# Hash-bucketed attention and a channel mix on one core: the third pair's q and k turned by TensorE, written PSUM banks, and a new written sequence

## The chip, the cores and the metric

The kernel runs on one core of a Trainium2 chip. The core has five engines that work side by side and wait for each other by semaphores: TensorE (PE in the profile; its weight loads are listed apart as PEld), VectorE (DVE), ScalarE (ACT), GpSimd (POOL), and SyncE (SP), which here only issues DMA transfers. The metric is the time of one execution in microseconds (us) on the device; smaller is better.

## The reference

Two blocks follow each other. First an attention whose mask comes from a hash: each row of q and k is projected on 6 random directions, the 6 signs make a bucket number, and a query sees only the keys of its own bucket. Then a channel mix with a token shift, a squared ReLU layer and a sigmoid gate.

```python
# q, k, v: (4, 8, 768, 64); proj: (64, 6); x: (4, 768, 512); w_k: (512, 1024), w_v: (1024, 512), w_r: (512, 512)
q_bits = einsum('bhsd,dk->bhsk', q, proj) > 0;  k_bits = the same of k
mask   = bucket(q_bits)[:, :, :, None] == bucket(k_bits)[:, :, None, :]
attn   = softmax(where(mask, q @ k.T / 8, -1e9));  x = heads side by side of attn @ v
x_prev = x shifted by one position, zero first
xk = mu_k * x + (1 - mu_k) * x_prev;  xr = mu_r * x + (1 - mu_r) * x_prev
out = sigmoid(xr @ w_r) * (maximum(xk @ w_k, 0) ** 2 @ w_v)
```

## The kernel before

The 32 heads are worked in 16 pairs, n = 0 to 15; four pairs make one batch b, and behind each batch its channel mix follows (`add_moe`). For a pair:

- *Loads* (`add_load`). q, k and v of both heads come from DRAM by SP's queue, three buffers each (ldq, ldv).
- *Preparation of q and k.* Each fp32 number becomes a half-precision "hi" (times 4) and the remainder "lo", side by side in 128 columns: hi on DVE, ACT or POOL (L554 to L556, L616 to L618), lo on DVE (L559, L621). The block must then be turned, so that these 128 columns lie on the partitions. There are two ways. `add_prep` (pairs 2 to 15) issues two DMA transposes on SP's queue (L563, tr). `add_prep_first` (pairs named in FIRSTS, 0 and 1) works each head and side apart: hi and lo of 384 columns, six transposes on PE into PSUM (L635, t), and a copy of 768 columns out of PSUM by DVE or ACT (L639, evt).
- *Sign rows.* PE multiplies with the projection (L587, bits), DVE takes the signs out of PSUM (L591, bx), and small DMAs put them as extra rows into the turned q and k (L599, row): two DMAs for pairs 1 to 3, four for the later ones. Pair 0 does without the DMAs: PE writes its sign products at the right partitions (L657, b) and DVE or ACT puts them into place (L663, L665, beb). With these rows, equal buckets add a constant to the score, which the exponential's bias takes off again, so unequal buckets vanish.
- *Scores* (`add_scores`). A pair has nine steps of 1024 score columns, each in two PSUM banks: PE (L708, sc), then the exponential on ACT (L712, exp). Three such double banks exist. Steps 5 to 8 are of the second head, 0 to 3 of the first, step 4 of both.
- *Times v* (`add_pv`, L736 and L741, oo): six groups of 12 matmuls per pair; DVE divides by the sum (rc, ob). For pairs 0 to 7 v is cast (va) and a sum of its rows is made in three additions (vsum, vsumb, vsumc) on DVE or POOL; later pairs subtract the mean of v (L528, mean).
- *Turn and mix* (`add_mix`): the result is turned by PE or by a DMA transpose (ot, otd), shifted (xs, xj), and mixed on DVE (df, xka, xk, xra, xr).

The channel mix of a batch has 16 blocks of the first layer (L859, kp), a ReLU on ACT or DVE (L864, L866), a square on DVE (L869), six gate blocks (L884, r, then a tanh on ACT, L887) and six blocks of the second layer (L896, v), whose product with the gate DVE makes (L903, os) before it is stored (L907, st). The very last block is made and stored in two halves of 256 columns.

What sets the order: every step is an entry of a plan with its engine, and ORDER is one written list of all entries (1386). Each engine works its own entries strictly in the order of that list. WHERE names the engine of those that can go to several. `schedule` walks the list, and for each step that needs PSUM it picks the bank that its estimates see free first, out of 0 to 5 in pairs for scores and 7 to 3 for single ones. Waits between engines follow from the data. The 512 values of mu_k and mu_r are loaded one by one into their columns (L422).

Of the kernel before, what the change touches and what calls it, by code (L numbers as in the profile page):

```python
# [16 lines left out]

LAG = {"PE": 0.21, "ACT": 0.21, "DVE": 0.15, "POOL": 0.18, "SP": 1.8, "GQ": 2.0}
# [17 lines left out]
def R(kind, n):  # L36
# [99 lines left out]
class Plan:  # L136
# [7 lines left out]
    def add(self, eng, dur, prio, fn, r=(), w=(), take=None, give=(), lag=None, name="", at=0.0, svc=0.0, off=None, tr=0, port=0, land=1.5):  # L144
# [31 lines left out]
        self.ops.append(o)  # L176
        return o

    def sequence(self):
        if ORDER:  # L180
            return [self.ops[i] for i in ORDER]
        left = {o.i: len(o.deps) for o in self.ops}
        heap = [(o.prio, o.i) for o in self.ops if not left[o.i]]
        heapq.heapify(heap)
        seq = []
        while heap:
# [73 lines left out]
def kernel(  # L260
# [13 lines left out]
    nc = tc.nc  # L274
# [690 lines left out]
```

## Time and profile before

| | |
|---|---|
| median of 3 runs | 250.7 us (248.66 to 250.73) |
| span of the profiled execution, first to last instruction (no other time of it is given) | 251.3 us |
| PE busy | 236.9 us (94%) |
| DVE busy | 195.4 us (78%) |
| ACT busy | 179.1 us (71%) |
| POOL busy | 27.9 us (11%) |
| DMA packets' time, share of 16 engines, main queue | 72.8% |

Busy time says how long an engine worked on something, not that it worked at its peak. A line Lxxx is a line of the kernel. In the lists of groups, an instruction is named by line, engine and operation, then what it writes and reads with partitions x elements, then how often; after the bar its busy time, the mean of one in ns, and the idle time of its engine before it with what ended that. In a timeline row the first number is the start, the second the length, and the bracket says how long the engine stood idle before and what released it. SPq is SP's queue of DMA issues. The granted clock of PE is given as a share of full speed, 1.00 being full.

### The profile page before, as it was taken

The page shows a single profiled execution, that of the slowest core. Times are in us where ns is not written, and L with a number is a line of the kernel's source. Part 1 is how long each engine was busy: PE and PEld are TensorE (multiplying, and loading weights), DVE is VectorE, ACT ScalarE, POOL GpSimd, SP SyncE. Part 2 cuts the span into 40 slices and gives each one's busy share as a digit, 9 for nine tenths or more (in the row PEclk, how much of TensorE's full clock was granted, in tenths as well). Part 3 has the DMA queues.
Part 4 walks back from the last instruction along what each step waited for, and adds up shares of the span by engine and source line. Part 5 has one row for each costly group of instructions (what it writes and reads, how often), then busy time and mean ns, then how long its engine had stood idle before and what let it go on. Part 6 is the DMA issues. An engine that isn't in the chain of part 4 may idle for free.

```text
span 251.3 us, 6510 instructions
## 1 busy us (share of the span) xinstructions
PE 236.9 (94%) x2609; PEld 147.6 (59%) x2609; DVE 195.4 (78%) x471; ACT 179.1 (71%) x225; POOL 27.9 (11%) x73
## 2 busy tenths in 40 slices
PE   6886799999799998999999999999999999999993
PEld 2444578876566655666467566655865654545442
DVE  3795679889788889898998999899787878376322
ACT  5596689999799978996878899988787223332220
POOL 5002240541302031100001100100000000000000
PEclk9799799999999999999999999999999999999998
DMA  6999999999989999999999996793231030022223
GB/s 187 308 178 251 220 215 191 267 249 189 213 292 241 204 293 292 273 201 269 184 333 186 184 185 158 210 230 57 90 64 44 0 128 28 13 83 86 83 85 125
DMA packets 75194, 44.56 MB, mean 177 GB/s; under 512 B 55524, under 2 KB 70172, under 8 KB 75164
## 3 DMA queue, kind: packets, MB, share of 16 engines
q1 hardware_dynamic: 74028, 44.15, 72.8%
q8 instruction: 20, 0.33, 0.6%
q10 hardware_dynamic: 1136, 0.01, 0.3%
q14 instruction: 10, 0.08, 0.1%
HBM read 24.12 MB, written 6.29 MB: 121 GB/s over the span
## 4 chain that ended last, share of the span: by engine, by line
PE 75%; DMA 11%; DVE 8%; SPq 3%; ACT 1%; issue 1%; DVEq 0%
PE ps_all L708 19%; PE ps_all L896 17%; PE ps_all L859 13%; PE ps_all L741 12%; PE ps_all L884 8%; DMA nat<-in_k_dram 5%; PE ps_all L587 4%; DMA nat<-in_q_dram 3%; DMA a<-bx 2%; DMA os<-in_moe_w_k_dram 1%; DVE nh L559 1%; DVE nh L556 1%; PE ps_all L736 1%; ACT pt L712 1%; PE ps_all L794 1%
## 5 line engine op out<-in xcount | busy, mean ns | idle before, releaser
L712 ACT ACTIVATE pt<-ps_all 128x1024 bf16<-128x1024 f32 x144 | 138.8, 1040 | 21.1 <-PE ps_all L708 19.8
L708 PE MATMUL ps_all<-a 128*128 128x512 f16 (+3 forms) x408 | 80.6, 318 | 5.1 <-DMA a<-bx 3.9
L708 PEld LDWEIGHTS <-a 128*128 128x128 f16 x408 | 35.3, 98 | 26.7 <-DMA a<-bx 4.7
L859 PE MATMUL ps_all<-xk,wk 128*128 128x384 bf16 x256 | 49.0, 326 | 0.9 <-DVE kr L866 0.9
L896 PE MATMUL ps_all<-wv,k 128*128 128x512 bf16 (+1 forms) x200 | 45.9, 370 | 0.6 <-DVE os L903 0.6
L741 PEld LDWEIGHTS <-pt 128*128 128x128 bf16 x1152 | 42.1, 98 | 6.9 <-issue 1.1
L741 PE MATMUL ps_all<-va,pt 128*128 128x65 bf16 x1152 | 43.9, 194 | 0.0
L859 PEld LDWEIGHTS <-wk 128*128 128x128 bf16 x256 | 24.5, 98 | 17.6 <-issue 1.6
L896 PEld LDWEIGHTS <-k 128*128 128x128 bf16 x200 | 19.4, 98 | 20.6 <-issue 0.7
L864 ACT ACTIVATE kr<-ps_all 128x384 bf16<-128x384 f32 x33 | 15.8, 493 | 19.2 <-DVE k L869 12.7
L887 ACT ACTIVATE rs<-ps_all 128x512 f32<-128x512 f32 x24 | 14.2, 603 | 20.9 <-PE ps_all L884 19.0
L559 DVE SCALAR_TENSOR_TENSOR nh<-nat,nh 128x768 f16<-128x768 f32 x28 | 27.3, 976 | 1.1 <-ACT nh L554 0.6
L903 DVE SCALAR_TENSOR_TENSOR os<-rs,ps_all 128x512 f32<-128x512 f32 (+1 forms) x25 | 16.5, 662 | 14.7 <-PE ps_all L896 9.9
L869 DVE TENSOR_TENSOR k<-kr 128x384 bf16<-128x384 bf16 x64 | 21.5, 350 | 3.7 <-ACT kr L864 3.5
L884 PE MATMUL ps_all<-wr,xr 128*128 128x512 bf16 x96 | 23.8, 379 | 0.0
L866 DVE TENSOR_SCALAR kr<-ps_all 128x384 bf16<-128x384 f32 x31 | 17.1, 555 | 8.3 <-PE ps_all L859 6.6
L758 DVE TENSOR_TENSOR ob<-ps_all,rc 128x384 bf16<-128x384 f32 (+1 forms) x36 | 18.3, 511 | 1.0
L884 PEld LDWEIGHTS <-xr 128*128 128x128 bf16 x96 | 9.0, 98 | 10.0 <-ACT kr L864 0.3
L587 PE MATMUL ps_all<-a,p0g 128*32 128x256 f16 (+1 forms) x180 | 13.4, 276 | 1.3 <-DMA a<-nh 1.3
L556 DVE TENSOR_SCALAR nh<-nat 128x768 f16<-128x768 f32 x22 | 12.3, 557 | 3.0 <-DMA nat<-in_q_dram 2.5
L587 PE MATMUL ps_all<-a,p1g 128*32 128x256 f16 (+1 forms) x180 | 12.9, 273 | 0.0
L841 DVE TENSOR_TENSOR xr<-tm,xt 128x768 bf16<-128x768 f16 (+1 forms) x18 | 9.4, 520 | 0.4
(94 smaller groups left out, 187.4 us busy)
## 6 DMA issues: line engine op xcount, KB each, us to landing
vn<-in_v_dram SPq DMA_DIRECT2D x16, 384.0 KB
out_dram<-os SPq DMA_DIRECT2D x23, 256.0 KB
nat<-in_k_dram SPq DMA_DIRECT2D x15, 384.0 KB
nat<-in_q_dram SPq DMA_DIRECT2D x15, 384.0 KB
wst<-in_moe_w_k_dram SPq DMA_DIRECT2D x2, 512.0 KB
wst<-in_moe_w_r_dram SPq DMA_DIRECT2D x2, 512.0 KB
wst<-in_moe_w_v_dram SPq DMA_DIRECT2D x2, 512.0 KB
a<-bx SPq DMA_DIRECT2D x48, 9.0 KB
```

The lines of the kernel that those rows point to most:

```text
L559: nc.vector.scalar_tensor_tensor(out=nh[:, :, D:P], in0=nat.rearrange("p j (c d) -> p (j c) d", d=D), scalar=QS, in1=nh[:, :, 0:D], op0=AL ...
L587: nc.tensor.matmul(ps[g_ * wid : (g_ + 1) * wid, 0:FW], w_[:, m_ - 1 - x : m_ - 1 - x + wid], a_t[sa][:, i, x % NFOLD * FW : (x % NFOLD + ...
L708: nc.tensor.matmul(ps[:, lo - s * STEP : hi - s * STEP], side_a["k"][sa][:, j, jc * P : (jc + 1) * P], side_a["q"][sa][:, j, q0 : q0 + hi ...
L712: nc.scalar.activation(out=pt_t[sp][:, s * STEP : (s + 1) * STEP], in_=ps_t[plan.slot[nm]], func=AF.Exp, bias=EBIAS, scale=ESC)
L741: nc.tensor.matmul(oo[:, (ic - c0) * 65 : (ic - c0) * 65 + 65], pt_t[sp][:, o : o + P], va_t[sa][:, j, jc, 0 : D + 1], start=(not uc and i ...
L758: nc.vector.tensor_tensor(out=ob_t[so][:, c0:c1, j * D : (j + 1) * D], in0=oo[:, :, 0:D], in1=rc_t[sr][:, 1, c0:c1].unsqueeze(2).to_broadc ...
L859: nc.tensor.matmul(ps[:, 0:HALF], wk_sb[:, d, fc * P : (fc + 1) * P], xk_t[mx[d]][:, h * HALF : (h + 1) * HALF], start=(d == 0), stop=(d = ...
L866: nc.vector.tensor_scalar(out=kr_t[sk], in0=sm(nm)[:, 0:HALF], scalar1=0.5 ** 0.5, scalar2=0.0, op0=ALU.mult, op1=ALU.max)
L869: nc.vector.tensor_tensor(out=k2_t[s2][:, h * HALF : (h + 1) * HALF], in0=kr_t[sk], in1=kr_t[sk], op=ALU.mult)
L884: nc.tensor.matmul(sm(nr), xr_t[mx[d]][:, c * P : (c + 1) * P], wr_sb[:, d, :], start=(d == 0), stop=(d == NDC - 1))
L896: nc.tensor.matmul(sm(nv)[:, lo:hi], k2_t[(b * NFC + fc) % NK2][:, c * P : (c + 1) * P], wv_sb[:, fc, lo:hi], start=(fc == 0), stop=(fc == ...
L903: nc.vector.scalar_tensor_tensor(out=os_t[so][:, lo:hi], in0=rs_t[s1][:, lo:hi], scalar=1.0, in1=sm(nv)[:, lo:hi], op0=ALU.add, op1=ALU.mult)
```

## The change

- FIRSTS becomes (0, 1, 2): pair 2's q and k are prepared by `add_prep_first` too. Two DMA transposes, two whole hi and two whole lo go; four hi and four lo of 384 columns, four groups of six PE transposes and four copies out of PSUM come.
- mu_k and mu_r are loaded as eight rows of 128 values, turned by one PE matmul with an 8 x 8 identity (made on POOL), and taken out of PSUM by one DVE instruction, in place of two loads of single values and two DVE instructions.
- SLOT names the PSUM bank of every operation; `schedule` only looks it up. Single operations may now lie in banks 0 to 7.
- ORDER is new (1397 entries), and so is the engine of many entries (WHERE). POOL has 103 entries in place of 67, among them most of the v sums and twelve casts of q or k; ACT has 217 in place of 227, DVE 437 in place of 455, PE 464 in place of 459, SP 176 in place of 178.
- The plan's durations and times of some entries change, which nothing reads any more. STEPS, ROWD, ROW_ACT and NWARM2 are options, all empty or zero. The second half of the last block is declared to follow the first (nv, 0).

How some lists begin or end, by the names above, before and then after:

```
PE  t0k10 t0q01 t0q00 t0q10 t0k01 t0k00 b0k10 b0q10 b0k00 b0k01 t1k10 b0q00 sc0_6 sc0_8 b0q01 t1q00 sc0_7 t1k00 sc0_5 t1q10 sc0_3 sc0_2 bits1 sc0_1 sc0_4 sc0_0 bits2 sc1_0 ...
PE  t0k10 t0q10 b0k10 t0q01 t0q00 b0q10 t0k00 t0k01 b0q01 sc0_7 sc0_6 b0q00 b0k00 sc0_5 t1q10 b0k01 t1q00 t1k00 t1k10 sc0_3 sc0_4 bits1 sc0_2 t2k10 sc0_1 t2q00 t2k00 t2q10 sc0_8 sc0_0 bits2 sc1_8 ...
DVE hi0k1 lo0k1 lo0q0 lo0q1 hi0k0 lo0k0 evt0q01 evt0q00 hi1k1 evt0k00 lo1k1 lo1k0 hi2q lo2q beb0q10 ...
DVE hi0k1 lo0k1 hi0q1 lo0q1 evt0k10 lo0q0 evt0q10 lo0k0 evt0q01 hi1q0 evt0q00 beb0q10 lo1q1 beb0q01 lo1q0 hi2q1 vsum0 hi1k1 lo1k1 vsum0b lo1k0 evt1q10 beb0q00 evt1k00 evt1k10 hi3q lo2k1 va1 lo2k0 bx1 lo2q0 evt2k10 lo2q1 evt2q00 evt2k00 evt2q10 ...
SP  ldq0k1 ldq0q0 ldq0q1 ldq0k0 ldq1k ldq2q ldq2k ldq1q ldq3q ldq3k tr2 ldq5q tr2 ldv0 ldq4q ldq4k row1 row1 ldv1 ldv2 row2 row2 tr3 tr3 ...
SP  ldq0k1 ldq0q1 ldq0q0 ldq0k0 ldq1q ldv0 ldq2q ldq1k ldq3q ldq2k ldv1 ldq4q ldv2 ldq3k ldq4k ldv3 row1 row1 ldv4 ldq5k ldq5q ldq6q row2 row2 tr3 tr3 tr4 tr4 ...
PE  ... r3_3 r3_5 v3_4 v3_5 (first half, 2 groups) v3_5 (second half, 2 groups)
PE  ... v3_5 (first half, 1) r3_3 v3_5 (first half, 2) r3_4 r3_5 v3_5 (second half, 2 groups) v3_4 (2 groups)
```

The diff, without the lists:

```diff
+BANKS = {"sc": 2, "s3": 3, "sm": 1}
-    FIRSTS = (0, 1)
+    FIRSTS = (0, 1, 2)
+    STEPS = {}
+    NWARM2 = 0
+    ROWD = ()
...
     def schedule(self):
...
+        used, held = set(), {}
+        order = [self.ops[i] for i in ORDER]
         for o in order:
             if o.take is not None:
-                choices = [(max(t, *(bank_free[b] for b in bs)), k, i, bs) for k, (i, bs) in enumerate(choices) if not any(used[b] for b in bs)]
-                t, _, self.slot[name], bs = min(choices)
+                name, size = o.take[1], BANKS[o.take[0]]
+                self.slot[name] = SLOT[name]
...
-    for t, src, key in ((muk, moe_mu_k, "muk"), (mur, moe_mu_r, "mur")):
-        def f_mu(t=t, src=src):
-            with nc.allow_non_contiguous_dma(reason="512 values"):
-                nc.scalar.dma_start(out=t, in_=src.rearrange("(c p) -> p c", p=P))
+    add("POOL", 0.3, -2.2, lambda: make_identity(nc, id8), w=["id8"], name="id8")
+    for i_, src in enumerate((moe_mu_k, moe_mu_r)):
+        add("ACT", 0.42, -19.0, lambda i_=i_, src=src: nc.scalar.dma_start(out=mu8[i_ * NDC : (i_ + 1) * NDC, :], in_=src.rearrange("(c p) -> c p", p=P)),
+            w=[("mu8", i_)], at=0.75, svc=0.05, off=1.5, land=1.05, name=f"ldmu{i_}")
+    add("PE", 0.12, 1.0, lambda: nc.tensor.matmul(sm("mu")[:, 0 : 2 * NDC], mu8, id8, start=True, stop=True),
+        r=["id8", ("mu8", 0), ("mu8", 1)], w=[("mu",)], take=("sm", "mu", 0), name="mu")
+    add("DVE", 0.08, 1.3, lambda: nc.vector.tensor_scalar(out=mu_t, in0=sm("mu")[:, 0 : 2 * NDC], scalar1=-1.0, scalar2=None, op0=ALU.add),
+        r=[("mu",)], w=["muk", "mur"], give=["mu"], name="muv")
...
-                        r=[("wv", fc) for fc in range(4 * g, 4 * g + 4)] + [...],
+                        r=[("wv", fc) for fc in range(4 * g, 4 * g + 4)] + [...] + ([(nv, 0)] if lo and g == 0 else []),
```

More of the change, by code (lines that the diff above doesn't have):

```diff
@@ L177, in add @@
         return o
[L179 to L186, printed above, removed]
-            o = self.ops[heapq.heappop(heap)[1]]
-            seq.append(o)
-            for s in o.succ:
-                left[s] -= 1
-                if not left[s]:
-                    heapq.heappush(heap, (self.ops[s].prio, s))
-        return seq
@@ L195, in moved @@
-    @staticmethod
-    def moved(t, work):
-        return t + work * (1.25 if t < 9.3 else 1.0)
-    def schedule(self):
-        free = {e: 0.0 for e in ("PE", "ACT", "DVE", "POOL", "SP")}
-        bank_free = [0.0] * 8
-        used = [False] * 8
-        count = {"sc": 0, "sm": 0, "moe": 0}
-        held = {}
-        dma_free = tr_free = after = 0.0
-        port = [0.0, 0.0]
-        queue = []
-        order = self.sequence()
+    def schedule(self):
+        used, held = set(), {}
+        order = [self.ops[i] for i in ORDER]
@@ L209, in schedule @@
         for o in order:
-            e = "POOL" if o.eng == "GQ" else o.eng
-            if o.svc and o.eng != "GQ":
-                queue.append(o)
-            t = max([free[e], o.at] + [queue[-9].vis if o.svc and o.eng != "GQ" and len(queue) > 8 else 0.0] + [self.ops[d].own if self.ops[d].eng == o.eng and not self.ops[d].svc else self.ops[d].vis for d in o.deps])
             if o.take is not None:
-                cls, name, moe = o.take
-                if count[cls] >= self.most[cls] or (moe and count["moe"] >= self.moe_most):
+                name, size = o.take[1], BANKS[o.take[0]]
@@ L221, in schedule @@
-                held[name] = (cls, bs, moe)
-                for b in bs:
-                    used[b] = True
-                count[cls] += 1
-                count["moe"] += moe
-            o.start = t
-            dur = o.dur
-            if o.port:
-                dur += max(0.0, port[e == "DVE"] - t)
-                port[e != "DVE"] = t + dur
-            if e == "SP":
-                dur += after
-                after = 0.3 * o.tr
-            if o.tr:
-                dma_free += 0.5 * (dma_free > t)
-                dur = max(dur, dma_free - 1.0 - t, tr_free + 0.1 - t)
@@ L237, in schedule @@
-            o.took = dur
-            free[e] = t + dur
-            lag = o.lag
-            if o.svc:
-                first = max(t + o.off, dma_free)
-                dma_free = self.moved(first, o.svc)
-                lag = max(0.9, dma_free + o.land - t - dur)
-                if o.tr:
-                    tr_free = dma_free
-            o.own = t + dur + 0.1 * (e in ("DVE", "ACT"))
-            o.vis = t + dur + lag
-            for name in o.give:
-                cls, bs, moe = held.pop(name)
-                for b in bs:
-                    used[b] = False
-                    bank_free[b] = o.vis
-                count[cls] -= 1
-                count["moe"] -= moe
@@ L255, in schedule @@
-        self.end = max(o.start + o.took for o in order)
+                used |= held[name]
+            for name in o.give:
+                used -= held.pop(name)
         return order
```

75 lines of the change are left out of this document (46 added, 29 removed), and 200 rows, old and new, of tables (ORDER, SLOT, WHERE).

## The prediction, made before the result was known

> **What bounds the kernel now.** I read the page's busy shares first, then three stretches, then what TensorE (PE) waited for.
>
> ```profile
> PE 236.9 (94%) x2609; PEld 147.6 (59%) x2609; DVE 195.4 (78%) x471; ACT 179.1 (71%) x225; POOL 27.9 (11%) x73
> ...
> 18.00:22.70 4.70, 4.70 (x59) 3.13 (x56) 3.68 (x6) 4.36 (x6) 0.00 (x0) 1.00 1.07 287
> 22.70:26.60 3.90, 0.02 (x2) 0.00 (x0) 1.58 (x5) 0.62 (x1) 1.67 (x2) 1.00 0.81 240
> 26.60:32.80 6.20, 6.17 (x71) 4.29 (x72) 3.59 (x6) 4.28 (x5) 1.08 (x2) 0.72 0.99 186
> ...
> 32.40:60.00 27.60, 27.59 (x485) 21.81 (x487) 23.97 (x63) 27.53 (x30) 8.86 (x18) 1.00 1.00 224
> 60.00:180.00 120.00, 117.39 (x1460) 74.62 (x1453) 106.99 (x264) 103.28 (x123) 12.21 (x26) 1.00 0.96 220
> ...
> PE ps_all L708 <- DMA a<-bx: 3.9, 1, 3.9
> ...
> PE ps_all L587 <- DMA a<-nh: 1.3, 2, 1.0
> ...
> PE ps_all L859 <- DVE kr L866: 0.9, 1, 0.9
> ```
>
> In a stretch, the numbers are its length, then busy time of PE, weight loads, DVE, ACT and POOL, then granted clock, DMA share and GB/s. PE is the bound: of the 120 us from 60 to 180 it is busy 117.39. From 32.4 to 60 ACT (27.53 of 27.60) is as full as PE. So no gain is to be had where PE is full, except by less PE work, and the change adds some. What can be won is PE's waits, and the largest stands at 22.7: 3.9 us in which the scores of the second pair wait for the sign rows (a<-bx). Behind it the granted clock is 0.72 for 6.2 us, so another 0.28 x 6.2 = 1.7 us of PE work is lost. The waits of 0.4 to 1.0 us between 12 and 18 left the clock at 1.00:
>
> ```profile
> 12.00:18.00 6.00, 4.50 (x38) 2.58 (x37) 5.81 (x12) 5.38 (x7) 0.00 (x0) 1.00 0.86 164
> ...
> 9.12 0.36 DVE L618 TENSOR_SCALAR nh<-nat 128x384 f16<-128x384 f32 x1 [1.51 <-DMA nat<-in_k_dram]
> 10.59 0.56 DVE L556 TENSOR_SCALAR nh<-nat 128x768 f16<-128x768 f32 x1
> 11.18 0.96 DVE L559 SCALAR_TENSOR_TENSOR nh<-nat,nh 128x768 f16<-128x768 f32 x1
> 12.17 0.95 DVE L665 TENSOR_SCALAR a<-ps_all 6x768 uint16<-6x768 uint16 x1
> ...
> 13.18 1.03 PE L708 MATMUL ps_all<-a 128*128 128x512 f16 x6 [0.99 <-DVE a L665]
> 26.63 1.70 PE L708 MATMUL ps_all<-a 128*128 128x512 f16 x7 [3.91 <-DMA a<-bx]
> ...
> 12.17 1.55 SPq L563 DMA_TRANSPOSE a<-nh  x1
> 15.62 2.04 SPq L563 DMA_TRANSPOSE a<-nh  x1
> 20.45 2.36 SPq L599 DMA_DIRECT2D a<-bx  x2
> ...
> L599 SPq DMA_DIRECT2D a<-bx x54: 721/752/1562, 20.4 to 177.4; - x54
> ```
>
> **The first scores** (start 13.18). They wait for the sign bits of the first pair's q, written by DVE at 12.17, and that DVE instruction stands behind the cast and remainder of the third pair's q (10.59 and 11.18). In the new sequence those two are gone from there; ahead of the sign bits stand the second pair's q cast and one 384-wide copy. That cast needs the fifth load, which landed at 9.12 (then k, now q). So 9.12 + 0.36 + 0.35 + 0.95 = 10.8: scores start 2.4 us sooner.
>
> **The second pair's scores** (start 26.63). From there DVE's written list sets the pace. Up to the rows' input (bx1) it holds six 384-wide remainders, two 384-wide sign copies, two 384-wide casts, three 768-wide copies, a 768 cast of q, one of v, and two v sums. With these rows:
>
> ```profile
> L621 DVE SCALAR_TENSOR_TENSOR nh<-nat,nh 128x384 f16<-128x384 f32 x8 | 4.4, 560 | 0.9 <-ACT nh L616 0.8
> L639 DVE COPY a<-ps_all 128x768 f16<-128x768 f16 x2 | 1.0, 552 | 0.0
> L509 DVE TENSOR_TENSOR vt<-va 128x390 f32<-128x390 bf16 x7 | 3.9, 557 | 0.0
> L512 DVE TENSOR_TENSOR vt<-vt 128x130 f32<-128x130 f32 x4 | 1.2, 294 | 2.3 <-POOL vt L509 2.2
> L591 DVE TENSOR_SCALAR bx<-ps_all 128x256 uint16<-128x256 uint16 x15 | 6.3, 421 | 3.8 <-PE ps_all L587 3.0 <-ACT pt L712 0.6
> ...
> 34.41 0.51 PE L794 MATMUL ps_all<-idb,ob 128*128 128x128 bf16 x6
> 34.75 1.15 PE L708 MATMUL ps_all<-a 128*128 128x128 f16 x8
> ...
> 35.91 1.43 PE ps_all L587 x24
> 41.18 0.44 PE ps_all L708 x4
> 99.73 0.77 PE ps_all L587 x24
> 101.05 0.65 PE ps_all L859 x4
> ```
>
> 6 x 0.56 + 2 x 0.555 (as the 384-wide copy out of PSUM of L866, below) + 2 x 0.36 + 3 x 0.55 + 2 x 0.56 + 0.557 + 0.29 = 8.8; bx1 starts at 10.8 + 8.8 = 19.6 and ends at 20.0. Then two remainders and four copies of the third pair: 6 x 0.55 = 3.3, to 23.3; PE's bits2 (24 matmuls, 1.43 us in the chain of waits, whose rows are the last four) to 24.7. DVE instructions overlap a little (two of L639, 552 ns each, are busy 1.0 us together): over some 24 of them at least 1 us less, 23.7. PE itself has less in between: after bits1 (ends about 18.8) four score steps of 0.44 and the third pair's transposes, 4 x 0.34 (six of L794 start at 34.41, what follows them at 34.75), end before 22. The added PE work, 24 transposes or 1.4 us, thus lies in a wait. The rows can end later than that: bx1 at 19.5 and two median issues of 0.75 make 21.0. Before, 3.8 us passed from their issue's end (22.81) to the scores, with ten loads and two transposes ahead; now twelve loads and no transpose are. Between 2 us and that 3.8 I take 3.1, which gives 24.1, **2.5 us sooner** than 26.63. Bounds: 23.2, if the overlap is twice as large; 26.6, if the first row's issue takes its 1.56 again and the landing longer.
>
> **The clock.** By the same walk PE's longest single wait there is about 0.9 us, for the second pair's k remainder, of the kind that left 1.00 between 12 and 18. So the **1.7 us** go too; the other bound is nothing.
>
> Against this speaks a sentence of the Trainium skill (TensorE: Matmul & The Clock Gate, Part 4: PE-mode transpose): transposes do not count as PE-busy for the clock gate, so filling the wait with them would not keep the clock. In this trace transposes among matmuls from 14.57 to 17 ran at 1.00, and none runs alone for 3 us; it is a rival below with a small chance.
>
> **Middle, 24 to 240.** Counts by engine, from the two lists: POOL goes from 67 to 103 operations (13 more first v sums, 9 more second and third ones, 8 whole and 4 half q/k casts, 2 weight casts; small ones left out). ACT loses 6 relus, 4 casts, 2 weight casts. DVE loses 22 v sums and 6 casts, and gains 6 relus and 6 copies.
>
> ```profile
> L509 POOL TENSOR_TENSOR vt<-va 128x390 f32<-128x390 bf16 x1 | 0.8, 847 | 0.1
> L512 POOL TENSOR_TENSOR vt<-vt 128x130 f32<-128x130 f32 x4 | 1.7, 436 | 11.7 <-DVE vt L509 11.7
> L501 POOL CAST va<-vn 128x768 bf16<-128x768 f32 x6 | 5.6, 930 | 25.6 <-DMA vn<-in_v_dram 19.3 <-PE ps_all L741 6.1 <-PE ps_all L859 0.2
> L866 DVE TENSOR_SCALAR kr<-ps_all 128x384 bf16<-128x384 f32 x31 | 17.1, 555 | 8.3 <-PE ps_all L859 6.6 <-issue 0.4
> L559 DVE SCALAR_TENSOR_TENSOR nh<-nat,nh x28: 947/955/1459, 11.2 to 160.3; 128x768 f16<-128x768 f32 x28
> ```
>
> POOL: 13 x 0.85 + 9 x 0.44 + 10 x 0.93 + 2 x 1.24 = 27 us more (casts at the 0.93 of the cast row, by width; at the two-operand rate of L509, 0.847/390 us, the ten would be 1.7 each and the sum 34). DVE: 13 x 0.557 + 9 x 0.29 + 6 x 0.557 - 6 x 0.555 - 6 x 0.5 = 7 us less; ACT some 8 less. None of that is PE's time; it is slack, and I give it the 0.9 us wait for L866. Against it, the sequence now issues the transposes of pairs 7 and 8 in one block of four, after four weight loads instead of two. The last of them leaves two issues, 4.1 us by the 2.04 above, after the second; PE has 3.4 us between (bits7 0.77, two first-layer blocks of 0.65, three score steps of 0.44). I keep the old 1.3 us wait for transposes and add **0.5**; bounds: -1.3 (all hidden) and +4 (two more transposes uncovered). The loading vectors mu, now turned by one small matmul, add 0.2 on PE (more than one transpose's 0.06, less than six's 0.34).
>
> Costed at nothing: the options that the diff adds are empty, so the score step stays 1024 wide and no row takes another queue; the written banks only name which read a block has to wait for, and with three score pairs and five single banks as before I see no row that would price another choice; the second head's turn at PE comes first in both lists for most pairs. ACT hides the two turned mu loads: they are issued on its queue between instructions, and mu is needed only when the first mixing starts.
>
> **The end.** The sequence ends differently.
>
> ```profile
> 245.35 0.60 ACT L887 ACTIVATE rs<-ps_all 128x512 f32<-128x512 f32 x1 [0.81 <-DVE os L903]
> 245.67 0.69 DVE L903 SCALAR_TENSOR_TENSOR os<-rs,ps_all 128x512 f32<-128x512 f32 x1 [0.41 <-PE ps_all L896]
> 246.60 0.42 DVE L903 SCALAR_TENSOR_TENSOR os<-rs,ps_all 128x256 f32<-128x256 f32 x1 [0.24 <-PE ps_all L896]
> 247.07 1.03 PE L896 MATMUL ps_all<-wv,k 128*128 128x256 bf16 x8 [0.57 <-DVE os L903]
> ```
>
> Before, the second half of the last block waits 0.57 us until DVE has read the first half out of the same bank. Now that second half follows r3_5 directly on PE: r3_5, then ACT's tanh 0.60, then os 0.42, with hand-overs of 0.03, 0.03 and 0.05, make a wait of 1.13. And the last block is a whole one: os 0.69 instead of 0.42, a store of 256 instead of 128 KB (0.45 at the 287 GB/s of 18 to 22.7; nothing, if latency alone counts). I take 0.56 + 0.27 + 0.4 = **1.2 us** lost; bounds 0.6 and 1.8.
>
> **The sum**: -2.5 - 1.7 - 0.9 + 0.5 + 0.2 + 1.2 = -3.2. (The 2.4 us of the first scores are not a term of their own: they are in the 24.1.) The profiled execution's span is 251.3, 0.6 above the median of 250.7; I apply the difference to the median: **247.5 us**. About 1% (2.5 us) is what a measurement of this kernel can tell from no change. The own range of this case, with the bounds of its steps, is 245 to 249.3.
>
> **Rivals.**
> - *The wait only moves* (0.16). The second pair's rows land late again, or its bits wait for casts now on POOL (hi1q1, hi1k0), which DVE's remainders follow in order. Then the 2.5 and the 1.7 are not won: 247.5 + 4.2 = 251.7. For it: loads fill the queue (share 1.07 just before). Against: no transposes ahead.
> - *Vector becomes the bound; slower* (0.14). An operation on POOL and one on DVE stretch each other: L559 took 1.459 at most against 0.955 while POOL cast v at 27.6. From 60 to 180 DVE is busy 106.99 of 120; with 5 us freed there and, by the lists, 18 of the 27 new POOL us falling there, full blocking makes 107 - 5 + 18 = 120. From that point on DVE's own waits for PE, some 6 us (L866 alone 6.6 over the whole span), come on top: 247.5 + 6 = 253.5. Against: most of the 28 L559 stayed near 0.955. The Trainium skill (SBUF — State Buffer, SBUF: two separate sides) has such a rule, one of the two holds a shared port for its whole instruction and the other blocks; the stretched rows agree that it happens.
> - *More slack than counted* (0.16). Second pair at 23.2 and all transposes hidden: 247.5 - 0.9 - 1.3 - 0.5 = 244.8.
> - *Transposes do not hold the clock* (0.05): 247.5 + 1.7 = 249.2.
>
> **Chances.** Forecast 0.49, of which two thirds lie under 248.2 (1% under the median): faster 0.34 + 0.16 = 0.50. Within 1%: 0.15 + 0.05 + 0.14 (of the moved wait) = 0.34. Slower: 0.14 + 0.02 = 0.16. The range leaves out most of the slow rival and the best of the fast one: 244.0 to 252.5.
>
> **What would show it.** Right: first scores near 10.8 and those of pair two near 24; no L708 wait on a<-bx over 1 us; clock 1.00 from 24 to 36; an L896 wait on os of about 1.1 us and a last store later after PE. Wrong: L559 or L837 well over their medians on average; PE waits on POOL or L621 above 1 us; bits8 waiting more than 2 us for a<-nh.

## The result and the profile after

The changed kernel takes **258.7 us** (median of four executions, 258.13 to 262.10) against 249.8 for the kernel before in the same comparison: a ratio of **1.042, interval 1.034 to 1.049**. It is slower by some 9 to 10 us where I had forecast 3 us less. (The ratios here leave out executions that took over 1.5% longer than the fastest of the same kernel; the medians hold them, so the two can differ, mostly by some tenths of a per cent.)

Something on the base first. In every execution that lists both, the time lies 1.7 to 2.1 us above the span. So the profile that the forecast read (span 251.3) is of an execution of about 253.1 us, longer than every timed one then (248.66 to 250.73). I had a second profile taken of the unchanged kernel (run `again`, below: span 247.8, time 249.73), and compare with that one from here on. The 8.5 us between the spans 247.8 and 256.3 are what is to be explained.

The busy times of the whole span, the second profile of before first, then the changed kernel:

```profile
PE 235.7 (95%) x2609; PEld 147.4 (59%) x2609; DVE 194.7 (79%) x471; ACT 179.0 (72%) x225; POOL 27.5 (11%) x73
```

```profile
PE 238.2 (93%) x2618; PEld 148.2 (58%) x2635; DVE 197.5 (77%) x453; ACT 172.1 (67%) x215; POOL 77.3 (30%) x110
```

VectorE has 18 operations fewer and is busy 2.8 us longer; POOL has 37 more and is busy 50 us longer.

Stretches of the kernel before, second profile (length, then busy time of PE, weight loads, DVE, ACT, POOL, then granted clock, DMA share, GB/s):

```profile
6.00:12.00 6.00, 3.90 (x27) 2.21 (x25) 4.25 (x11) 2.70 (x5) 0.56 (x4) 0.80 1.03 335
12.00:24.00 12.00, 11.15 (x104) 6.52 (x102) 10.10 (x18) 10.69 (x13) 0.66 (x1) 0.96 0.85 203
24.00:36.00 12.00, 10.28 (x144) 7.45 (x145) 9.13 (x18) 9.71 (x12) 4.96 (x11) 1.00 1.10 231
...
0.00:60.00 60.00, 53.44 (x724) 36.93 (x725) 46.76 (x106) 50.05 (x58) 16.51 (x49) 0.97 0.99 236
60.00:180.00 120.00, 118.22 (x1467) 75.84 (x1465) 106.19 (x265) 104.09 (x124) 10.66 (x23) 1.00 0.89 215
```

The same stretches of the changed kernel:

```profile
6.00:12.00 6.00, 5.03 (x32) 2.19 (x30) 4.99 (x11) 3.98 (x8) 2.63 (x8) 1.00 1.07 360
12.00:24.00 12.00, 10.08 (x116) 7.01 (x117) 11.87 (x23) 9.45 (x12) 10.76 (x17) 1.00 0.70 237
24.00:36.00 12.00, 11.22 (x161) 8.07 (x158) 8.47 (x15) 10.72 (x12) 4.82 (x7) 1.00 1.11 228
...
0.00:60.00 60.00, 53.35 (x709) 36.42 (x710) 46.20 (x99) 48.21 (x56) 33.12 (x62) 1.00 0.93 235
60.00:180.00 120.00, 113.94 (x1433) 73.34 (x1440) 101.50 (x232) 104.13 (x124) 43.94 (x48) 1.00 0.87 200
```

Read three things. The clock is 1.00 throughout, so that part of the start came as forecast; but up to 60 us PE is busy for the same 53.4 us in both, and in the changed kernel that has to hold 24 transposes and the mu product more (the higher clock is worth about 1.2 us of it, see `again` below). The start is thus no gain. From 60 to 180 PE idles 6.1 us (120 - 113.94) instead of 1.8: 4.3 us lost in the middle. And VectorE is less busy there than before (101.50 against 106.19), while POOL is busy four times as long.

PE's transposes of q and k, the second profile of before first, then the changed kernel with its mu product:

```profile
L635 PE MATMUL ps_all<-idh,nh 128*128 128x128 f16 x48 | 4.5, 241 | 2.7 <-DVE nh L621 2.7
```

```profile
L630 PE MATMUL ps_all<-idh,nh 128*128 128x128 f16 x72 | 6.6, 235 | 2.2 <-DVE nh L616 2.0
...
L405 PE MATMUL ps_all<-id,tm 8*128 8x8 f32 x2 | 0.4, 262 | 0.0
```

PE's waits of the changed kernel (what it waited for: us in total, times, longest), and below them the first score steps of the first two pairs and the end in the timeline (start, length, in brackets the idle time before and its releaser):

```profile
PE ps_all L703 <- DMA a<-bx: 2.7, 5, 1.0
PE ps_all L630 <- DVE nh L616: 2.0, 4, 0.8
PE ps_all L854 <- DVE ob L753: 1.8, 1, 1.8
...
PE ps_all L570 <- POOL p0g L399: 1.1, 1, 1.1
PE ps_all L891 <- DVE os L898: 1.1, 1, 1.1
...
PE ps_all L570 <- DMA a<-nh: 0.6, 1, 0.6
PE ps_all L511 <- POOL vs L498: 0.5, 1, 0.5
```

```profile
10.29 1.02 PE L703 MATMUL ps_all<-a 128*128 128x512 f16 x5 [0.64 <-DVE a L660]
...
24.25 1.04 PE L703 MATMUL ps_all<-a 128*128 128x256 f16 x5
...
249.74 2.76 PE L891 MATMUL ps_all<-wv,k 128*128 128x256 bf16 x15 [1.14 <-DVE os L898]
...
252.60 0.69 DVE L898 SCALAR_TENSOR_TENSOR os<-rs,ps_all 128x512 f32<-128x512 f32 x1 [1.36 <-PE ps_all L891]
```

No single wait is large. The loss is many small ones, of which the largest, 1.8 us at 140.9, shows how they arise: PE waits for DVE's division (ob), DVE waits 2.5 us for a DMA transpose of the older ob, and that transpose was issued on SP's queue only at 134.91, behind loads and rows. Two waits are for POOL itself, where before had none. The longer of them shows best what a full POOL does:

```profile
34.93 2.13 POOL L539 TENSOR_SCALAR nh<-nat 128x768 f16<-128x768 f32 x1
37.14 1.62 POOL L492 TENSOR_TENSOR vt<-va 128x390 f32<-128x390 bf16 x1
...
39.33 0.20 POOL L399 COPY p0g<-p 128x6 f16<-128x6 f16 x1
...
39.58 0.29 PE L570 MATMUL ps_all<-a,p0g 128*32 128x256 f16 x4 [1.15 <-POOL p0g L399]
```

PE's sign product needs the projection in the layout p0g. That copy takes POOL 0.20 us, but in POOL's list it stands behind a cast of 2.13 us and a v sum of 1.62, and PE waits 1.15 us for it.

Groups of operations on DVE and POOL (count | busy, mean ns of one | idle before), the changed kernel first, then the second profile of the kernel before:

```profile
L539 POOL TENSOR_SCALAR nh<-nat 128x768 f16<-128x768 f32 x8 | 17.4, 2176 | 25.5 <-DMA nat<-in_q_dram 10.4 <-DVE mc L524 8.7 <-DMA a<-nh 6.1
L492 POOL TENSOR_TENSOR vt<-vn 128x384 f32<-128x384 f32 x8 | 9.6, 1195 | 29.9 <-DMA vn<-in_v_dram 29.8
...
L492 POOL TENSOR_TENSOR vt<-va 128x390 f32<-128x390 bf16 x6 | 6.5, 1084 | 0.8 <-DVE va L484 0.5
L484 POOL CAST va<-vn 128x768 bf16<-128x768 f32 x6 | 5.7, 957 | 6.9 <-DMA vn<-in_v_dram 5.4 <-PE ps_all L736 1.5
L613 POOL TENSOR_SCALAR nh<-nat 128x384 f16<-128x384 f32 x4 | 5.3, 1327 | 3.5 <-DMA nat<-in_q_dram 2.2 <-DMA nat<-in_k_dram 1.1
...
L542 DVE SCALAR_TENSOR_TENSOR nh<-nat,nh 128x768 f16<-128x768 f32 x26 | 26.4, 1018 | 0.3 <-POOL nh L539 0.2
L864 DVE TENSOR_TENSOR k<-kr 128x384 bf16<-128x384 bf16 x64 | 24.3, 399 | 4.2 <-ACT kr L859 3.8
```

```profile
L559 DVE SCALAR_TENSOR_TENSOR nh<-nat,nh 128x768 f16<-128x768 f32 x28 | 27.3, 975 | 1.1 <-ACT nh L554 0.6
L869 DVE TENSOR_TENSOR k<-kr 128x384 bf16<-128x384 bf16 x64 | 21.6, 352 | 3.7 <-ACT kr L864 3.5
```

A q or k cast on POOL takes 2.18 us where DVE needs 0.56, and DVE's own operations are longer beside it: 64 squares at 399 ns instead of 352 are 3.0 us alone.

### The profile page after: what moved, and what is told of

Read it like the earlier page. It is cut to its first block, busy times and chain, and to the rows that moved or that the text cites. A ratio compares the mean times of both kernels' runs of the same rounds, so it can differ in the third digit from the quotient of the medians.

```text
span 256.3 us, 6565 instructions
## 1 busy us (share of the span) xinstructions
PE 238.2 (93%) x2618; PEld 148.2 (58%) x2635; DVE 197.5 (77%) x453; ACT 172.1 (67%) x215; POOL 77.3 (30%) x110
## 4 chain that ended last, share of the span: by engine, by line
PE 56%; DVE 16%; DMA 10%; issue 6%; ACT 4%; POOL 4%; SPq 2%; DVEq 0%; POOLq 0%; ACTq 0%
PE ps_all L891 14%; PE ps_all L854 12%; PE ps_all L703 10%; PE ps_all L736 8%; PE ps_all L879 7%; DMA a<-nh 5%; ACT pt L707 4%; PE ps_all L570 3%; DVE nh L542 3%; DMA xt<-ob 2%; DMA nat<-in_q_dram 2%; DVE nh L616 2%; POOL nh L539 2%; DMA k<-in_moe_w_v_dram 1%; DVE nh L539 1%
## 5 line engine op out<-in xcount | busy, mean ns | idle before, releaser
L736 PEld LDWEIGHTS <-pt 128*128 128x128 bf16 x1152 | 43.5, 97 | 8.7 <-issue 0.9
L703 PEld LDWEIGHTS <-a 128*128 128x128 f16 x408 | 34.2, 97 | 23.8 <-issue 4.6
L736 PE MATMUL ps_all<-va,pt 128*128 128x65 bf16 x1152 | 45.5, 193 | 0.1
L882 ACT ACTIVATE rs<-ps_all 128x512 f32<-128x512 f32 x24 | 14.2, 596 | 24.1 <-PE ps_all L879 19.9
L859 ACT ACTIVATE kr<-ps_all 128x384 bf16<-128x384 f32 x27 | 13.0, 490 | 21.8 <-PE ps_all L854 11.5
L864 DVE TENSOR_TENSOR k<-kr 128x384 bf16<-128x384 bf16 x64 | 24.3, 399 | 4.2 <-ACT kr L859 3.8
L542 DVE SCALAR_TENSOR_TENSOR nh<-nat,nh 128x768 f16<-128x768 f32 x26 | 26.4, 1018 | 0.3 <-POOL nh L539 0.2
L539 POOL TENSOR_SCALAR nh<-nat 128x768 f16<-128x768 f32 x8 | 17.4, 2176 | 25.5 <-DMA nat<-in_q_dram 10.4
L861 DVE TENSOR_SCALAR kr<-ps_all 128x384 bf16<-128x384 f32 x37 | 20.3, 553 | 5.9 <-PE ps_all L854 4.9
L492 POOL TENSOR_TENSOR vt<-vn 128x384 f32<-128x384 f32 x8 | 9.6, 1195 | 29.9 <-DMA vn<-in_v_dram 29.8
L879 PEld LDWEIGHTS <-xr 128*128 128x128 bf16 x96 | 9.3, 98 | 10.8 <-DVE xr L836 0.8
```

Of the source, the lines that this page charges most:

```text
L539: e.tensor_scalar(out=o, in0=x, scalar1=QS, scalar2=None, op0=ALU.mult)
L542: nc.vector.scalar_tensor_tensor(out=nh[:, :, D:P], in0=nat.rearrange("p j (c d) -> p (j c) d", d=D), scalar=QS, in1=nh[:, :, 0:D], op0=AL ...
L703: nc.tensor.matmul(ps[:, lo - s * w : hi - s * w], side_a["k"][sa][:, j, jc * P : (jc + 1) * P], side_a["q"][sa][:, j, q0 : q0 + hi - lo], ...
L736: nc.tensor.matmul(oo[:, (ic - c0) * 65 : (ic - c0) * 65 + 65], pt_t[sp][:, o : o + P], va_t[sa][:, j, jc, 0 : D + 1], start=(not uc and i ...
L861: nc.vector.tensor_scalar(out=kr_t[sk], in0=sm(nm)[:, 0:HALF], scalar1=0.5 ** 0.5, scalar2=0.0, op0=ALU.mult, op1=ALU.max)
L864: nc.vector.tensor_tensor(out=k2_t[s2][:, h * HALF : (h + 1) * HALF], in0=kr_t[sk], in1=kr_t[sk], op=ALU.mult)
```

## The experiments

Ratios are to the kernel before on the same chip in the same comparison; 0.01 is 2.5 us. Theory A was: POOL's long operations and their stretching of VectorE are the loss. Theory B: the written sequence, whatever engine does what. Theory C: turning the third pair on PE.

**again**: the kernel before, unchanged.

> The kernel before, unchanged, profiled a second time. Its first profiled execution had a span of 251.3 us; the changed kernel's 258.13 us has a span of 256.3, so a span lies about 1.8 us under the time, and 251.3 would be a time of 253.1, above all timed runs of the kernel before (248.66 to 250.73). Theory 'the profile was untypical': span 247 to 249, the wait of the second pair's scores for a<-bx clearly under 3.9 us or the clock behind it above 0.9, so that 2 to 4 of the 4.2 us that the forecast won at the start were not there to win. Rival 'typical': the wait is again 3.9 and the clock again 0.72, span 250 to 251.5.

Ratio 1.000 (0.996 to 1.004), median 249.7. The profile was untypical: span 247.8, and

```profile
25.41 1.46 PE L708 MATMUL ps_all<-a 128*128 128x512 f16 x7 [1.95 <-DMA a<-bx]
```

the wait was 1.95 us instead of 3.91, and behind it the clock was 1.00; low clock stood between 6 and 24 us, worth some 1.2 us (0.2 of 3.9 and 0.04 of 11.2).

**poolback** and **hiback**: the changed kernel with operations taken off POOL again.

```diff
 # poolback: 49 entries of v sums, v casts and, from the fourth pair on, q/k casts as in the kernel before
-    "vsum5": "POOL", "vsum5b": "POOL", "hi8q": "POOL", "hi13q": "POOL", ...
+    "vsum5": "DVE",  "vsum5b": "DVE",  "hi8q": "DVE",  "hi13q": "ACT", ...
 # hiback: only the 12 q/k casts that were on POOL
```

> The changed kernel with its written sequence and banks, but every v sum, every v cast and every q and k cast from the fourth pair on, on the engine that has it before (49 of 87 entries differ). POOL's busy time falls from 77 to some 45 us, VectorE's counts rise by about 10 us and its stretch shrinks. Theory A (POOL's slow casts and sums, and their stretching of VectorE, are the loss): 250 to 253 us, ratio to the kernel before 1.00 to 1.015. Theory B (the written sequence itself is the loss, whatever engine does what): 257 to 260, ratio 1.03 to 1.04.

> The changed kernel with only its 12 q and k casts on POOL (2.18 us for 128x768) given back to VectorE (8) and ScalarE (4); v sums stay on POOL. Theory A with the casts as the main part: 252 to 256 us. Theory A with the v sums as the main part, or theory B: 257 to 260.

poolback: **262.6 us, ratio 1.052 (1.043 to 1.061)**; hiback: 260.5, ratio 1.046 (1.034 to 1.058). Neither is faster than the change; poolback's median is 3.9 us longer. Its largest wait of PE was for a v sum, now on DVE:

```profile
PE ps_all L511 <- DVE vs L498: 2.7, 1, 2.7
```

The test wasn't clean for theory A: it freed POOL but loaded DVE and ACT in a sequence in which their entries had been placed without that work. (hiback also moved four casts of the start, where PE then waited 2.9 us for a remainder.)

**bpool**, **bvs**, **bhi**, **bpcut**: the same engines, the other way round, in the kernel before.

```diff
 # bpool: 45 entries as in the changed kernel; bvs: the 32 v sums alone; bhi: the 13 q/k casts alone
-    "vsum5": "DVE",  "vsum5b": "DVE",  "hi8q": "DVE",  "hi13q": "ACT", ...
+    "vsum5": "POOL", "vsum5b": "POOL", "hi8q": "POOL", "hi13q": "POOL", ...
 # bpcut: bpool, and on POOL only
+    E = 4                                # v sums, from the fifth pair on
+    o, x = o[:, 0:1, :], x[:, 0:1, :]    # q/k casts: 1 of 12 chunks
```

> The kernel before, in its own sequence, with the engines of the changed kernel for the v sums and for the q and k casts from the fourth pair on (45 entries differ; POOL 28 -> some 65 us). Theory A: 254 to 258 us, ratio 1.02 to 1.035, with VectorE's 128x768 remainder above 1.00 us on average. Theory B: 249 to 251.5, ratio 0.995 to 1.007.

> The kernel before, its own sequence, with only the v sums on the engines of the changed kernel (32 entries: 27 go to POOL, 5 come back). Both kinds together gave 256.7 us, ratio 1.030. If it goes by POOL's busy time, v sums hold half: 252.5 to 254, ratio 1.012 to 1.018. If the chain cast, remainder, transpose, rows is what counts, v sums cost little: 250 to 251.5.

> The kernel before, its own sequence, with only the q and k casts from the fourth pair on as in the changed kernel (13 entries, 8 of them to POOL at 2.15 us). By POOL's busy time: 252.5 to 254. If VectorE's remainders waiting for POOL's casts (8.1 us in the run with both kinds) are the cost: 255 to 257, ratio 1.022 to 1.03.

> Both kinds moved in the sequence of before, with POOL's casts cut to 1 of 12 chunks and its v sums from the fifth pair on to 4 of 64 columns (that part of the computation is left out). If the durations on POOL are the cost of the move: 248 to 251 us, ratio 0.993 to 1.005. If it is the order on POOL's queue and the added hand-overs, whatever an operation takes: 254 to 257.

bpool: **256.7 us, ratio 1.030 (1.021 to 1.039)**; bvs: 254.3, 1.017 (1.007 to 1.028); bhi: 253.9, 1.018 (1.009 to 1.026). So the move, with no other part of the change's sequence, costs 3%, each kind by itself about half of that. In bpool VectorE's remainders stood 8.1 us behind POOL's casts:

```profile
DVE nh L559 <- POOL nh L556: 8.1, 3, 3.7
```

But bpcut, with the durations on POOL cut, stayed at 255.4, **ratio 1.026 (1.017 to 1.036)**: in that sequence most of the cost, as far as the intervals tell, is not how long an operation takes. The wait above falls to 0.9 us there, and PE's waits stay. POOL, too, works its list in order, and what now stands on it queues behind entries that themselves wait:

```profile
POOL nh L562 <- DMA nat<-in_q_dram: 26.4, 4, 8.1
POOL xt L784 <- DVE tm L843: 24.5, 1, 24.5
POOL vt L511 <- DMA vn<-in_v_dram: 21.8, 6, 6.0
```

That this queueing is what delays DVE and PE in bpcut is argued from these rows, not shown by a run of its own. And it has a rival: the four runs did not move operations alone. In the kernel before, `schedule` picks PSUM banks by its estimates, and these go by the engine of each entry. By the kernels' own plans, 78 of the 339 blocks that need a bank lie in another one in bpool than before (48 in bvs, 76 in bhi), and bpcut has bpool's very banks. PE's waits for exponentials, first in `again`, then in bpool, then in bpcut:

```profile
PE ps_all L708 <- ACT pt L712: 0.3, 1, 0.3
```

```profile
PE ps_all L708 <- ACT pt L712: 3.4, 5, 1.2
PE ps_all L587 <- ACT pt L712: 1.2, 1, 1.2
```

```profile
PE ps_all L714 <- ACT pt L718: 3.6, 6, 1.2
PE ps_all L593 <- ACT pt L718: 1.2, 1, 1.2
```

Neither scores nor sign products read what an exponential writes, so these are waits for a bank to be read out. The sign product of 1.2 us is that of the eighth pair, which lies in bank 5 in these two runs and in bank 6 before. The waits are as long with the durations cut as without. How much of the 3% are the banks and how much the queue on POOL, no run shows.

Sequence and engines, set against each other (ratio to the kernel before):

| | engines of before | engines of the change |
|---|---|---|
| sequence of before | 1.000 | 1.030 (bpool) |
| sequence of the change | 1.052 (poolback) | 1.042 |

(The exchanged entries are nearly the same: v sums and q/k casts from the fourth pair on, in poolback the v casts too.) Each sequence has its lower number with the engines that it was written with, but the intervals of 1.042 and 1.052 overlap, and 1.030 holds other banks too. So theory A and theory B can't be told apart by exchanging engines: the two were chosen together. What can be taken away without unbalancing a list is the duration of an operation.

**short**, **shorthi**, **shortv**: the changed kernel with POOL's durations cut as in bpcut (both kinds, the 8 whole q/k casts, the v sums).

> The changed kernel, same sequence, engines and banks, but POOL's operations are cut: a v sum on POOL from the fifth pair on adds 4 of its 64 columns, a q or k cast on POOL from the fourth pair on turns 1 of its 12 chunks (the rest of the tile keeps older values, so that part of the computation is left out). POOL's busy time falls from 77 to some 40 us and its holding of VectorE with it; nothing else moves. Theory A (POOL's durations and their stretching of VectorE are the loss): 250 to 253.5 us, ratio 1.00 to 1.015, VectorE's 128x768 remainder back to 0.96 us on average. Theory B (the written sequence, with its queue of transfers, is the loss): 256 to 258.5, ratio 1.025 to 1.035.

> As the run with POOL's work cut, but only the 8 whole q and k casts on POOL are cut (1 of 12 chunks each, the rest of the computation of these casts is left out): some 14 of the 29.5 us. If the loss is POOL's own lateness in one chain (cast, remainder, transpose, rows), the casts hold the most of it: 254 to 255.5 us. If it is the stretching of VectorE, it goes by POOL's busy time, about half of 5.4 us: 255.5 to 256.5.

> The other half: only the v sums on POOL are cut (4 of 64 columns from the fifth pair on; that part of the sums is left out), some 16 of the 29.5 us. Stretching by busy time: 255.5 to 256.5. Lateness of the casts as the main part: 257 to 258.5.

short: **253.3 us, ratio 1.020 (1.009 to 1.032)**, against 1.042 (1.034 to 1.049) of the change: the intervals don't meet (barely), so in this sequence, with the same banks, POOL's durations are worth some 5 us. The ratio lies between what I expected by theory A (up to 1.015) and by theory B (from 1.025). Its rows:

```profile
PE 235.6 (94%) x2618; PEld 147.8 (59%) x2635; DVE 189.9 (75%) x453; ACT 171.9 (68%) x215; POOL 47.8 (19%) x110
...
L548 DVE SCALAR_TENSOR_TENSOR nh<-nat,nh 128x768 f16<-128x768 f32 x26 | 26.0, 1002 | 0.1
L870 DVE TENSOR_TENSOR k<-kr 128x384 bf16<-128x384 bf16 x64 | 21.5, 356 | 4.4 <-ACT kr L865 4.0
...
60.00:180.00 120.00, 115.42 (x1432) 74.53 (x1440) 96.95 (x238) 103.65 (x123) 19.16 (x45) 1.00 0.86 198
```

With POOL at 47.8 instead of 77.3 us, VectorE's busy time falls from 197.5 to 189.9, though its count is the same 453, and the squares are back at 356 ns. (The remainder at 1002 ns is not back at 0.96, as I had expected.) shorthi gives 254.7 (1.024, 1.017 to 1.031) and shortv 254.6 (1.021, 1.013 to 1.029): each half gives back nearly all that both do, so my expectation that the gain goes by busy time is wrong. Nor does it go by VectorE's stretch: VectorE's busy time falls by 3.4 us in shorthi (194.1), 4.6 in shortv (192.9) and 7.6 in short, which adds up, while the gains of 4.4, 5.2 and 5.3 us by the ratios don't, as far as intervals of 2 to 3 us either way tell. The 1.15 us wait for p0g fits the lateness on POOL: it is there with the casts uncut (shortv, 1.5) and isn't listed in short or shorthi. Which share the stretch has stays open. Of the 4.7 us between the spans of the change and of short (256.3 and 251.6), 2.1 are idle time of PE and 2.6 are busy time (238.2 and 235.6).

**hy24** and **hy70**: the changed kernel's order and engines up to 24 or 70 us, then the rest as before.

```diff
-ORDER = [ ...the changed kernel's list... ]
+ORDER = [ ...its entries up to the second pair's first scores (hy70: the first layer)...,
+          ...all others in the kernel before's order... ]
```

> The changed kernel up to the first scores of the second pair (third pair turned by PE, mu turned by PE, the new start), then what is left in the order and on the engines of the kernel before. Theory A and theory B both lose it all after 24 us, so 245 to 248 us, ratio 0.98 to 0.99, if the start's gain of the forecast is real; 249 to 250 (ratio 0.995 to 1.005) if the profile of before was untypical there. Theory C (the third pair by PE and the mu matmul cost it): 254 to 258, ratio 1.02 or more.

> The changed kernel's order and engines up to PE's first layer of the first block (about 70 us), then what is left in the order and on the engines of the kernel before. With the same join as the run cut at 24 us, which gave 254.6 us. If the loss of the middle arises before 70 us: 255 to 258. If it arises behind 70 us: 251 to 254.6.

hy24: median 254.6 us, ratio 1.017 (1.007 to 1.028); hy70: 256.8, 1.033 (1.024 to 1.043). The start alone, followed by before's rest, is slower than before. Part of that is the join: PE waits 1.7 us for a v sum that the list now reaches late. hy70 does not date the loss, only that it isn't all behind 70 us. Neither run is the changed kernel up to its join, for the banks were chosen anew: of 344 blocks, 230 lie in another bank than in the changed kernel in hy24 and 212 in hy70. It shows in hy70's waits of PE:

```profile
PE ps_all L732 <- ACT pt L736: 3.6, 7, 1.1
...
PE ps_all L659 <- DVE a L689: 1.9, 1, 1.9
```

The second stands at 15.14 and about half of the first between 31 and 47 us, where order and engines are still those of the changed kernel. The changed kernel's list of PE waits has none for an exponential. Up to 60 us the two still keep pace: the score step that waits for its rows starts at 59.76 in hy70 and at 59.43 in the changed kernel.

**third** and **third2**: the kernel before with two parts of the change alone, the third pair by PE and the mu product.

```diff
-    FIRSTS = (0, 1)
+    FIRSTS = (0, 1, 2)
 # DVE, third:  bx1 | hi2 lo2 x4 | copies x4 | bx2 | hi3 lo3 x2 | v sums of pair one | hi4 ...
 # DVE, third2: bx1 | hi2 lo2 x4 | copies x4 | v sums of pair one | hi3 lo3 | bx2 | hi3 lo3 | hi4 ...
```

> The kernel before, its order and engines, with two parts of the change alone: the third pair's q and k are turned by PE (its casts and remainders on VectorE behind the second pair's rows) and the mixing vectors by one small matmul. In the forecast's sum the first scores come 2.4 us sooner and the second pair's scores 2.5 us; against the kernel before's second profile (wait for a<-bx of 1.9 us instead of 3.9) about half of that is left: 248 to 250 us, ratio 0.99 to 1.00. If the added transposes (24, some 1.7 us of PE) find no wait to lie in, 251 to 253, ratio 1.005 to 1.015.

> The kernel before, its order and engines, with the third pair's q and k turned by PE and the mixing vectors by one matmul, as in the run before of this kind, but with the first pair's v sums ahead of the third pair's copies' followers, all four turns of the third pair ahead of the second pair's scores, and the second pair's rows ahead of the next load. The 4.0 us wait for the v sums and the turn queued behind the scores' wait go; the second pair's scores start near 22 us instead of 25.4. If the start's gain is real: 247 to 249.5 us, ratio 0.985 to 1.00. If VectorE's added copies (6 of 0.55 us) only move the wait to the third pair's rows: 250 to 252.

third was badly laid out: 257.4 us at the least, 260.6 in the median, PE waiting 4.0 us for the first pair's v sums, which I had left behind the third pair's work on DVE. third2 mended that and still gives, against 247 to 252 us expected, **254.7, ratio 1.026 (1.019 to 1.033)**, although its second pair's scores start 3.4 us sooner than in the second profile (25.41):

```profile
21.96 1.03 PE L732 MATMUL ps_all<-a 128*128 128x512 f16 x5
...
32.34 0.51 PE L818 MATMUL ps_all<-idb,ob 128*128 128x128 bf16 x6 [1.94 <-DVE ob L782]
...
0.00:60.00 60.00, 52.48 (x704) 37.16 (x705) 46.24 (x107) 47.84 (x56) 17.35 (x48) 0.97 0.81 212
```

The 3.4 us are spent again within ten: PE comes to the first pair's turn at 30.4 and waits until DVE, which is busy without a break from 18.0 to 34, has divided it. By 60 us PE has worked 1 us less than before, and more of it is added work. All but 15 of 339 blocks lie in the banks of before, so theory C holds in this list: the third pair by PE costs here, and does not gain. In the change's own sequence it was not tried alone.

**t2cut**: third2 with the third pair's 8 casts and remainders cut to 1 of 6 chunks.

> The second kernel with the third pair turned by PE in the sequence of before (254.7 us), but its 8 casts and remainders on VectorE do 1 of 6 chunks (the rest keeps older values, that part of the computation is left out): some 2.9 us less on VectorE between 18 and 22 us, about as much as turning by PE had added there; the 24 transposes of PE and the 4 copies stay. If VectorE's queue between 12 and 36 us is what takes the gain of the start back: 250.5 to 252.5 us. If PE's added transposes or the later rows of pairs three and four do: 254 to 255.5.

The four executions took 251.6, 252.0, 255.9 and 256.4 us. The ratio, 1.012 (1.002 to 1.022), goes by the two shorter ones; the median of all, 254.0, is hardly under third2's 254.7, and the interval overlaps third2's, which begins at 1.019. So whether taking some 3 us from VectorE gives anything back stays open, and with it whether VectorE's queue is what takes the gain of the start.

**tailb** and **shorttail**: the last blocks in before's order, in the changed kernel and in short.

```diff
-PE: v3_5  r3_4  r3_5  v3_5 v3_5  v3_4 v3_4
+PE: r3_4  r3_5  v3_4 v3_4  v3_5  v3_5 v3_5
```

> The changed kernel with the last blocks in the order of the kernel before (whole block 4 first, the two halves of block 5 last). The forecast's own term for the end, 1.2 us (a wait of 1.13 instead of 0.57, a longer last read and store): 257.0 to 257.8 us against 258.3 to 259.1. If the later store was hidden, 258 to 259.

> POOL's work cut as in the first run of that kind (parts of the v sums and of the q and k casts left out) and the last blocks in the order of the kernel before. If the two causes add: 253.3 - 1.2 = 252.1 us (251.5 to 252.7), and what is left to the kernel before, about 2 us, belongs to the start and the rest of the sequence. If the end's order only matters while the middle is late: 253 to 254.

tailb: 257.3 us, ratio 1.033 (1.027 to 1.038). That is 1.4 us under the change, about the size forecast, but the intervals overlap. shorttail: 254.1, ratio 1.023 (1.014 to 1.032), no less than short. Whether the two add stays open.

No version beat the kernel before.

## Why the prediction was wrong, step by step

- **The first scores and the second pair's scores: right in place, wrong in worth, and the second partly by luck.** Forecast 10.8 and 24.1; measured 10.29 and 24.25, no wait for a<-bx above 1.03 us, clock 1.00 from 24 to 36. The forecast let the second pair wait for its rows, issued by 21.0 and landed 3.1 us later (no row stood behind the lower bound of 2 us). Measured, the rows were issued by 21.28, and the scores don't wait for them at all: they follow bits2 (22.82) on PE without a gap. The path that the forecast had put at 23.7 set the start. And the -2.5 was taken against 26.63 in an execution that was itself some 3 us long; in the second profile those scores start at 25.41, which leaves 1.2. The 0.6 us by which I set the profile above the median compared a span with a time; like with like it was 253.1 against 250.7, so 2.4.
- **The clock, -1.7.** Regained as forecast, but of the second profile only some 1.2 us were there to regain, and not behind that wait. The rival that transposes don't hold the clock fell: 10.08 us of PE work between 12 and 24, transposes among it, ran at 1.00.
- **"The added PE work thus lies in a wait".** This failed, and with it the whole gain of the start: up to 60 us PE is busy 53.35 us against 53.44 and holds 24 transposes more. The added transposes take 2.1 us by the rows above, where I had 1.4, and the mu product 0.4, where I had 0.2. third2 shows that sooner scores are not worth their microseconds: the next thing that PE needs there (ob) comes from VectorE, which is busy without a break. I counted VectorE's work only up to bx1 and bx2 and called what came behind it slack.
- **The middle: "None of that is PE's time; it is slack". The step that failed most.** POOL's +27 us (34 by the other bound) became +50 (77.3 against 27.5). The casts, costed at 0.93 from the v cast, took 2.18, which makes 13 of the 23 us; the first v sums, costed at 0.85, took 1.08 to 1.20. And it was PE's time: in the written sequence the durations alone are worth 5 us (short), and in before's sequence the same move, with the banks that came with it, costs 3% (bpool). VectorE's -7 became +2.8 (197.5 against 194.7); 7.6 of these 9.8 us go with POOL's durations (short).
- **The block of four DMA transposes, +0.5 on top of 1.3.** Too large: the forecast 1.8 in all became 0.6 us of PE waits for a<-nh (0.9 in the second profile of before). The 0.9 us wait for L866 went, as forecast.
- **The written banks, costed at nothing.** The changed kernel's waits show no price for its own banks; but hy70, bpool and bpcut show that other banks can come with 4 to 5 us of waits for exponentials, so the reason given (no row that would price another choice) was too weak for a nothing.
- **The end, +1.2.** Right in each part: the wait 1.14 (forecast 1.13), the last read 0.69, and from the last matmul's end (252.50) to the end of the span 3.8 us, against 3.2 (248.10 to 251.3) before.
- **The rivals.** "Vector becomes the bound; slower" had the right sign and the right pair of engines, and 0.14. Its mechanism was half right: VectorE did stretch (7.6 us by short), but it never filled (101.50 of 120). PE lost its time in many small waits instead, which no engine's busy share shows. "More slack than counted" was as wrong as the forecast, for the same reason. "The wait only moves" had the worth of the start right (nothing), but not by late rows.

What the sum looks like from the second profile: of the 8.5 us between the spans, 6.0 are idle time of PE (18.1 us against 12.1) and 2.5 are busy time (238.2 against 235.7). The idle time is 0.1 up to 60 us, 4.3 from 60 to 180, and 1.6 behind, where the end's 1.2 lies. The 2.5 us of busy time are as much as the added transposes and the mu product take, but that doesn't settle it: short holds the same added work and is busy 235.6 us. By the ratios, POOL's durations are about half of the loss; the other half, 2% that short still has, is open. The written banks were not tried alone, and what the sequence costs by itself can't be had from these runs, since every exchange of engines in it also unbalances it.

## What to carry to other kernels

In a kernel whose engines each work a written list, an operation moved to an idle engine isn't free: cost it with a row of the same operation and types on that engine, add what it stretches on its neighbour and where it stands in the new queue, and then ask which short wait of the bound engine it feeds. Look, too, at what else moves with it: here a plan that picks banks by estimates picked others as soon as an engine changed. A start that comes sooner is worth only what the next engine in line can take up; follow its queue until the bound engine is late again. And set a profile's execution beside the timed runs before counting its waits as gains: a wait that stands at its full length in one execution alone isn't there to be won.

## What I had not expected of the hardware

On POOL the size doesn't tell the time. A plain cast of 128x768 from fp32 to bf16 took 0.96 us, a multiplication by a constant of the same size from fp32 to fp16 2.18, and half of that size 1.33; in the second profile of before DVE takes 0.56 for the same multiplication. The two whole-size operations differ in the output type and the layout too, and no run parts these. With POOL busy for 77.3 us instead of 27.5, DVE's squares in SBUF (128x384) went from 352 to 399 ns (back to 356 in short), and its ReLUs of the same size out of PSUM stayed where they were:

```profile
L861 DVE TENSOR_SCALAR kr<-ps_all 128x384 bf16<-128x384 f32 x37 | 20.3, 553 | 5.9 <-PE ps_all L854 4.9
```

In the second profile of before that same operation has a mean of 556 ns. The Trainium skill (SBUF — State Buffer, SBUF: two separate sides) puts such waiting down to a port that the two engines share and that one of them holds for a whole instruction; the rows agree that the squares, whose operands lie in SBUF, are hit and this operation isn't.
